# One queue for the reads of the transposed probabilities, and another place for the rounding of the mixed weights, in a fused attention and feed-forward kernel

## The chip, the cores and the metric

The kernel runs on one core of a Trainium2 chip. The metric is the time of one execution on the device, in microseconds, as the median of three runs: 532.76 us before the change, with runs from 532.27 to 533.12. All matrix products run on TensorE (PE). ScalarE (ACT), VectorE (DVE) and GpSimd (POOL) do the element-wise work, and SyncE (SP) issues most of the DMA transfers. ScalarE can issue transfers too, and does so in the kernel before.

## The reference

An attention with a global and a local window is followed by a gated feed-forward network of four weight matrices. In short (batch 4, 8 heads, 768 positions, 64 features a head; 8 global positions, a local window of 96):

```python
scores = matmul(q, k.T) / 8 + bias                      # bias = -slope(head) * distance
scores = where(is_global | is_local, scores, -1e9)      # local: 0 <= i - j < 96; global: j < 8
a = exp(scores - max(scores)); a = a / (sum(a) + 1e-9)
x = matmul(a, v)                                        # 4 x 8 x 768 x 64, laid out as 3072 x 512
h = ((x @ w1) * (x @ w2)) @ w3                          # 512 -> 1024 -> 1024
out = h @ w_out                                         # 1024 -> 512
```

## The kernel before

**Attention in 24 steps.** A step treats two head pairs of one block of 256 query positions; steps are counted from 0 to 23. In step s TensorE first makes a *visit*: the scores of step s (L488) and the products of the probabilities with the values of step s - 2 (L597). For each of the eight score tiles VectorE then subtracts the scores from the bias and takes the row extreme (L504), and ScalarE takes the exponential with the row sums (L505). These are the *rows* of the step. The scaling by the inverse sums follows: half of it on ScalarE (L521, four instructions a step) and half on VectorE (L523).

**The way of the probabilities.** The product with the values needs the probabilities transposed. VectorE transposes blocks of 32 x 32 (L558, four instructions a step), SyncE writes the result to device memory (`d`, L560, two transfers), and `back` (L568) reads it from there in four transfers into the tile `ph`, in an order that completes the transposition. Two of the four reads go out on SyncE's queue and two on ScalarE's. The reads of step s stand in step s + 1 in the program, and TensorE uses them in the visit of step s + 2. In the same place SyncE issues the loads for the next visit: keys and queries of step s + 1 (`qr`, L466) and values of step s - 1 (`vr`, L473). A buffer for a load comes free when TensorE has done the visit that used it, and SyncE waits for this with all that stands behind it in its queue.

**The feed-forward in slices.** TensorE's time between visits is filled with *slices* of `FeedForward.run`, a generator that the steps advance by fixed numbers (`SLICES`). For each eighth f of the 1024 features it makes two PSUM tiles, `m_f_0` and `m_f_1` (L220 to L222: weights and tokens are each split into a rounded high part and a rest, so one product takes three matmuls). ScalarE copies the first out of PSUM (L228), VectorE multiplies the second by it (L230), ScalarE rounds the product to its high part `gh` (L57), and VectorE subtracts to get the rest `gl` (L58). Then come the `o` tiles (L241 to L243), the copy of each out of PSUM (L251) and its store to the output (L252). All these PSUM tiles share two buffers: a tile can be begun when the tile before the last has been copied or multiplied out.

**The mixed weights.** The last part of the feed-forward (from about 400 us) is a Strassen product. It needs sums and differences of the weight blocks, which are prepared in the attention steps 7 to 22, one f in two steps: in an odd step `mix` forms them on GpSimd (L859, L862) into `tl`; in the following even step `round_off` rounds them on ScalarE to `th` (L867, 128 x 1024 elements) and subtracts on GpSimd (L869); and `keep` stores both to device memory (`tw`, L873, L874).

**What sets the order.** For the steps shown here the programs of TensorE, ScalarE, SyncE and GpSimd stand in the order in which the code is written. Only VectorE's order is made by a scheduler when the kernel is built, so it can change when another engine's code is moved. An instruction waits in its engine's queue for its inputs and for the buffer that it writes, with all behind it waiting too.

## Time and profile before

| | |
|---|---|
| median of three runs | 532.76 us (532.27 to 533.12) |
| the profiled execution | 532.92 us, of which the span of instructions is 531.2 us |
| TensorE matmuls (PE) | 520.4 us busy, 98% of the span, 4260 instructions |
| TensorE weight loads (PEld) | 414.1 us, beside the matmuls |
| VectorE (DVE) | 338.0 us, 64% |
| ScalarE (ACT) | 257.0 us, 48% |
| GpSimd (POOL) | 71.3 us, 13% |
| DMA | 107.7 MB, 203 GB/s in the mean |

A span is measured from the first to the last instruction of one profiled execution; the time of the execution is a little longer. Busy times are sums over the instructions of an engine. Times inside a trace count from the span's start. The granted TensorE clock stands at nine tenths or full speed in all 40 slices of the span, apart from one of eight tenths at the start.

Of the traffic in the attention steps, the page gives the median time from issue to landing: 3.4 us for the writes `d` (42 of them, 512 KB each), 6.7 us for the reads of `ph` on SyncE's queue and 6.2 us on ScalarE's (42 each, 160 KB), 4.5 us for the 16 `qr` loads of 624 KB and 6.1 us for the 17 `vr` loads of 512 KB.

### The profile page before, as it was taken

Reading aid. Unit: us, or ns where it says so; the run is one execution under the profiler, and the core shown is the slowest. Engines: PE = TensorE matmul, PEld = TensorE weight load, DVE = VectorE, ACT = ScalarE, POOL = GpSimd, SP = SyncE. Lnnn points to the kernel's source line nnn. Section 1 sums busy time; section 2 is a strip of 40 time slices with the busy share of each in tenths; the row PEclk is TensorE's granted clock in tenths of the full one; section 3 lists DMA queues with packets and bytes.
Section 4 is the critical chain, followed back from the end, with each engine's and each line's share of the span. In section 5 each row is a group of like instructions: output and inputs, shape, how many; then the busy total and the mean of one; then the engine's idle time right before and its main releaser. Section 6 shows DMA issues by size and latency. Waiting matters only on the chain.

```text
span 531.2 us, 11252 instructions
## 1 busy us (share of the span) xinstructions
PE 520.4 (98%) x4260; PEld 414.1 (78%) x4260; DVE 338.0 (64%) x906; ACT 257.0 (48%) x729; POOL 71.3 (13%) x87
## 2 busy tenths in 40 slices
PE   7999999999999999999999999999999999999996
PEld 3445468989988888888888888788888888888885
DVE  7999998976787576665767656677535433334400
ACT  0344776576676554546665554667424322222220
POOL 0000000000325050243214042412000000000000
PEclk9899999999999999999999999999999999999999
DMA  8977854477879765886767597988613322222031
GB/s 300 408 290 299 284 200 169 120 253 247 263 229 291 249 209 192 268 269 207 257 209 261 164 320 249 275 242 278 221 66 127 112 95 81 79 85 74 1 116 49
DMA packets 50653, 107.70 MB, mean 203 GB/s; under 512 B 4768, under 2 KB 28576, under 8 KB 50592
## 3 DMA queue, kind: packets, MB, share of 16 engines
q1 hardware_dynamic: 43056, 99.50, 54.3%
q10 hardware_dynamic: 7392, 6.88, 5.5%
q0 software_dynamic: 144, 0.52, 0.5%
q8 instruction: 35, 0.57, 0.4%
q14 instruction: 26, 0.21, 0.1%
HBM read 69.67 MB, written 36.70 MB: 200 GB/s over the span
## 4 chain that ended last, share of the span: by engine, by line
PE 84%; DVE 8%; DMA 4%; ACT 2%; issue 1%; SPq 0%; ACTq 0%; DVEq 0%
PE m L220 10%; PE m L221 9%; PE m L222 9%; PE a L948 8%; PE w L197 8%; PE o L241 6%; PE o L242 5%; PE o L243 5%; PE s L488 5%; PE v L597 5%; PE ob L968 4%; PE oa L968 4%; PE b L948 4%; PE c L948 2%; DVE t3s L164 2%; DMA ph<-d 2%
## 5 line engine op out<-in xcount | busy, mean ns | idle before, releaser
L220 PE MATMUL m<-xh,wqh 128*128 128x512 f32 (+1 forms) x320 | 113.3, 354 | 1.6 <-DVE ring_a L230 1.1
L221 PE MATMUL m<-xl,wqh 128*128 128x512 f32 (+1 forms) x320 | 111.0, 347 | 0.0
L222 PE MATMUL m<-xh,wql 128*128 128x512 f32 (+1 forms) x320 | 111.0, 347 | 0.0
L505 ACT ACTIVATE pr<-pr,mx 128x232 f32<-128x232 f32 (+1 forms) x192 | 88.1, 461 | 10.3 <-DVE mx L504 10.3
L220 PEld LDWEIGHTS m<-xh,wqh 128*128 128x128 f32 x320 | 60.5, 189 | 11.6 <-DVE ring_a L230 1.5
L504 DVE CUSTOM_DVE_ANT_0 pr<-s,biasw 128x232 f32<-128x232 f32 x160 | 54.0, 395 | 19.7 <-PE s L488 19.6
L222 PEld LDWEIGHTS m<-xh,wql 128*128 128x128 f32 x320 | 60.5, 189 | 7.6
L221 PEld LDWEIGHTS m<-xl,wqh 128*128 128x128 f32 x320 | 60.6, 189 | 7.1
L558 DVE STREAM_TRANSPOSE ph<-pr 128x512 f32<-128x512 f32 x84 | 49.1, 640 | 3.2 <-ACT pr L521 2.1
L241 PE MATMUL o<-wh,gh 128*128 128x512 f32 x128 | 50.8, 397 | 0.0
L243 PE MATMUL o<-wh,gl 128*128 128x512 f32 x128 | 49.9, 390 | 0.0
L242 PE MATMUL o<-wl,gh 128*128 128x512 f32 x128 | 49.9, 390 | 0.0
L57 ACT ACTIVATE gh<-ring_a 128x512 fp32r<-128x512 f32 x29 | 18.2, 629 | 50.8 <-DVE ring_a L230 48.0
L230 DVE TENSOR_TENSOR ring_a<-m,ring_a 128x512 f32<-128x512 f32 x32 | 21.8, 682 | 26.5 <-PE m L222 26.0
L869 POOL TENSOR_TENSOR tl<-tl,th 128x512 f32<-128x512 f32 x16 | 21.8, 1381 | 112.3 <-ACT th L867 112.3
L488 PE MATMUL s<-qr 64*64 64x168 f32 (+2 forms) x768 | 36.7, 299 | 0.0
L505 ACT ACTIVATION_READ_ACCUMULATOR pr<-pr,mx 128x1 f32 x192 | 36.1, 188 | 0.0
L597 PE MATMUL v<-ph,vr 64*64 64x64 f32 (+2 forms) x1208 | 34.5, 243 | 0.2 <-DMA ph<-d 0.2
L521 ACT ACTIVATE pr<-pr,sm 128x232 f32<-128x232 f32 (+1 forms) x84 | 33.2, 465 | 2.5 <-DVE sm L510 2.5
L597 PEld LDWEIGHTS v<-ph,vr 64*64 64x64 f32 (+1 forms) x1208 | 32.3, 133 | 1.7 <-DMA ph<-d 0.5
L197 PE MATMUL w<-wo,ta 128*128 128x512 f32 x64 | 30.2, 625 | 1.9 <-DVE ta L164 1.9
L523 DVE TENSOR_SCALAR pr<-pr,sm 128x232 f32<-128x232 f32 (+1 forms) x84 | 30.0, 398 | 1.3
(154 smaller groups left out, 850.3 us busy)
## 6 DMA issues: line engine op xcount, KB each, us to landing
d<-ph SPq DMA_DIRECT2D x42, 512.0 KB, 3.4
qr<-qk SPq DMA_DIRECT2D x16, 624.0 KB, 4.5
vr<-vx SPq DMA_DIRECT2D x17, 512.0 KB, 6.1
t<-tw SPq DMA_DIRECT2D x32, 256.0 KB, 3.0
ph<-d SPq DMA_DIRECT2D x42, 160.0 KB, 6.7
ph<-d ACTq DMA_DIRECT2D x42, 160.0 KB, 6.2
out_dram<-ring_o SPq DMA_DIRECT2D x24, 256.0 KB, 2.6
raw<-w3t SPq DMA_DIRECT2D x11, 512.0 KB, 9.6
```

The lines of the kernel that those rows point to most:

```text
L197: nc.tensor.matmul(ps, lhsT=x.bitcast(F32), rhs=self.wo[:, k].bitcast(F32), start=n == 0, stop=n == NFC - 1)
L220: nc.tensor.matmul(ps[:, z], lhsT=mh, rhs=xh[:, i], start=i == 0, stop=False)
L221: nc.tensor.matmul(ps[:, z], lhsT=mh, rhs=xl[:, i], start=False, stop=False)
L222: nc.tensor.matmul(ps[:, z], lhsT=ml, rhs=xh[:, i], start=False, stop=i == NCC - 1)
L241: nc.tensor.matmul(ps, lhsT=gh[:, f, ts], rhs=self.wh[:, f], start=f == 0, stop=False)
L242: nc.tensor.matmul(ps, lhsT=gh[:, f, ts], rhs=self.wl[:, f], start=False, stop=False)
L243: nc.tensor.matmul(ps, lhsT=gl[:, f, ts], rhs=self.wh[:, f], start=False, stop=f == NFC - 1)
L488: nc.tensor.matmul(ps[u][g * HQ:(g + 1) * HQ, j, cols], lhsT=m[:, q0:q0 + HQ], rhs=m[:, j * SLOT:][:, cols], start=True, stop=True)
L504: nc.vector.tensor_tensor_reduce(out=pr[:, j, u, w0:], in0=ps[u][:, j, w0:UW], in1=bias, scale=-SCALE, scalar=3.0e38, op0=ALU.add, op1=ALU ...
L505: nc.scalar.activation(pr[:, j, u, w0:], pr[:, j, u, w0:], AF.Exp, bias=m, scale=-1.0, accum_out=sm[:, j, u:u + 1])
L597: nc.tensor.matmul(uu[i][u * D:(u + 1) * D, j * P + q:j * P + q + n], lhsT=v[r], rhs=x[:, q // step:(q + n) // step][r], start=k == 0 and ...
L948: nc.tensor.matmul(ps, lhsT=a, rhs=b, start=first and k == 0 and i == 0, stop=k == HC - 1 and i == 2, skip_group_check=True)
```

## The change

Three things are done in the loop over the steps.

First, all four reads of `back` go out on SyncE's queue, and `back(s - 1)` stands ahead of the two `loads` instead of behind them. So in each step SyncE issues the reads of the transposed probabilities before anything else.

Second, `round_off` (ScalarE's rounding L867 and GpSimd's subtraction L869, in the even steps 8 to 22) stands behind `send`, which holds the transpositions, and no longer ahead of the first two slices of the step, which hold a copy L228 or L251 out of PSUM.

Third, `keep`, the stores of the mixed weights, stands one step later: in the odd step that follows, ahead of its slices, and so ahead of the `mix` that forms the next weights.

```diff
@@ back(s)
         for b, m0 in enumerate((1, 0, 3, 2)):
             ms = slice(m0, m0 + 5)
-            (nc.sync, nc.scalar)[b // 2].dma_start(out=x[b * BK:(b + 1) * BK].rearrange("r k a u c -> r (k a) (u c)")[:, ms], in_=d[:, :, :, b].rearrange("k a r e -> r (k a) e")[:, ms])
+            nc.sync.dma_start(out=x[b * BK:(b + 1) * BK].rearrange("r k a u c -> r (k a) (u c)")[:, ms], in_=d[:, :, :, b].rearrange("k a r e -> r (k a) e")[:, ms])
         phs[s] = x
@@ for s in range(SWAP + 1, n)
                     if i == 0 and uu is not None:
                         take(sv, uu)
+                back(s - 1)
                 loads(s + 1, vals=False)
                 loads(s - 1, keys=False)
-                back(s - 1)
-                if 0 <= s - MIX < 2 * NFC and (s - MIX) % 2:
-                    round_off()
+                f, late = divmod(s - MIX, 2)
+                if mixed and not late:
+                    keep()
                 slices(2)
                 for p, r in zip(pairs(s), rs):
                     softmax(*p, *r, nc.vector)
                 send(s, rs)
-                if mixed:
-                    keep()
-                if 0 <= s - MIX < 2 * NFC and (s - MIX) % 2 == 0:
-                    mix((s - MIX) // 2)
+                if mixed and late:
+                    round_off()
+                elif 0 <= f < NFC and not late:
+                    mix(f)
                 slices(SLICES[s] - 2)
```

What this does to the order of the instructions shows at four places. A row gives the line, the operation, what is written and read, the shape and how often it stands in a row; a number in a name counts tiles.

ScalarE in step 20, before, from the last exponentials on (`pr_0` and `pr_1` are the two head pairs of the step, `m_0_0` the first PSUM tile of the next group):

```order
L505 ACTIVATE pr_1_3770,sm_1_3772<-pr_1_3770,mx_1_3771 128x232 x4
L568 DMA ph_2_3651<-d_2_3652 32x5x256 x2
L867 ACTIVATE th<-tl 128x1024
L228 ACTIVATE ring_a<-m_0_0_3707 128x512
L521 ACTIVATE pr_0_3758<-pr_0_3758,sm_0_3760 128x232 x2
L521 ACTIVATE pr_1_3770<-pr_1_3770,sm_1_3772 128x232 x2
L57 ACTIVATE gh_3705<-ring_a 128x512
```

ScalarE at the same place, changed:

```order
L505 ACTIVATE pr_1_3770,sm_1_3772<-pr_1_3770,mx_1_3771 128x232 x4
L228 ACTIVATE ring_a<-m_0_0_3707 128x512
L521 ACTIVATE pr_0_3758<-pr_0_3758,sm_0_3760 128x232 x2
L521 ACTIVATE pr_1_3770<-pr_1_3770,sm_1_3772 128x232 x2
L867 ACTIVATE th<-tl 128x1024
L57 ACTIVATE gh_3705<-ring_a 128x512
L228 ACTIVATE ring_a<-m_1_0_3835 128x512
```

The two reads have left this queue, and the rounding L867 has moved from ahead of the copy L228 to behind the four scalings L521.

VectorE in the same step, before, from its half of the scalings on to the first row of step 21 (`pr_2`):

```order
L523 TENSOR_SCALAR pr_1_3770<-pr_1_3770,sm_1_3772 128x232 x2
L230 TENSOR_TENSOR ring_a<-m_0_1_3799,ring_a 128x512
L558 STREAM_TRANSPOSE ph_0_3818<-pr_0_3758 128x4x128 x2
L558 STREAM_TRANSPOSE ph_0_3818<-pr_1_3770 128x4x128 x2
L58 TENSOR_TENSOR gl_3706<-ring_a,gh_3705 128x512
L230 TENSOR_TENSOR ring_a<-m_1_1_3851,ring_a 128x512
L504 ISA pr_2_3911,mx_2_3912<-s_108,biasw 128x232
L504 ISA mx_2_3912 128x1
L58 TENSOR_TENSOR gl_3706<-ring_a,gh_3705 128x512
L504 ISA pr_2_3911,mx_2_3912<-s_109,biasw 128x232
```

VectorE at the same place, changed:

```order
L523 TENSOR_SCALAR pr_1_3770<-pr_1_3770,sm_1_3772 128x232 x2
L558 STREAM_TRANSPOSE ph_0_3815<-pr_0_3758 128x4x128 x2
L558 STREAM_TRANSPOSE ph_0_3815<-pr_1_3770 128x4x128 x2
L230 TENSOR_TENSOR ring_a<-m_0_1_3796,ring_a 128x512
L58 TENSOR_TENSOR gl_3706<-ring_a,gh_3705 128x512
L230 TENSOR_TENSOR ring_a<-m_1_1_3849,ring_a 128x512
L58 TENSOR_TENSOR gl_3706<-ring_a,gh_3705 128x512
L504 ISA pr_2_3909,mx_2_3910<-s_108,biasw 128x232
L504 ISA mx_2_3910 128x1
```

The product L230 of the tile `m_0_1` has moved from ahead of the four transpositions L558 to behind them. The second L58, which reads the ScalarE rounding L57 of the tile `m_1_1`, has moved from behind the first L504 of step 21 to ahead of it. The scheduler makes the first of these moves in steps 6, 10, 17, 20 and 21, and the second at the starts of the visits' rows in steps 6, 8, 17 and 21.

VectorE at the end of step 16 and the start of step 17 (`pr_2`), before:

```order
L230 TENSOR_TENSOR ring_a<-m_5_1_3189,ring_a 128x512
L504 ISA pr_2_3255,mx_2_3256<-s_108,biasw 128x232
L504 ISA mx_2_3256 128x1
L58 TENSOR_TENSOR gl_2812<-ring_a,gh_2811 128x512
L504 ISA pr_2_3255,mx_2_3256<-s_109,biasw 128x232
```

The same place, changed:

```order
L230 TENSOR_TENSOR ring_a<-m_5_1_3187,ring_a 128x512
L58 TENSOR_TENSOR gl_2810<-ring_a,gh_2809 128x512
L504 ISA pr_2_3253,mx_2_3254<-s_108,biasw 128x232
L504 ISA mx_2_3254 128x1
L504 ISA pr_2_3253,mx_2_3254<-s_109,biasw 128x232
```

The L58 of step 16 has moved past the first L504 of step 17 here as well.

SyncE from the writes of step 7 to the loads of step 8's end, before (`d` is the transposed tile in device memory, `ph` where it is read to, `tw` the stored mixed weights):

```order
L560 DMA d_2_1584<-ph_2_1583 128x1024 x2
L466 DMA qr_2_1724<-qk 128x1248
L473 DMA vr_2_1726<-vx 128x2x384
L568 DMA ph_2_1583<-d_2_1584 32x5x256 x2
L560 DMA d_0_1761<-ph_0_1760 128x1024 x2
L873 DMA tw<-th 128x1024
L874 DMA tw<-tl 128x1024
L252 DMA out_dram<-ring_o 128x512
L466 DMA qr_0_1865<-qk 128x1248
L473 DMA vr_0_1867<-vx 128x1024
L568 DMA ph_0_1760<-d_0_1761 32x5x256 x2
```

SyncE at the same place, changed:

```order
L560 DMA d_2_1584<-ph_2_1583 128x1024 x2
L568 DMA ph_2_1583<-d_2_1584 32x5x256 x4
L466 DMA qr_2_1728<-qk 128x1248
L473 DMA vr_2_1730<-vx 128x2x384
L560 DMA d_0_1758<-ph_0_1757 128x1024 x2
L252 DMA out_dram<-ring_o 128x512
L568 DMA ph_0_1757<-d_0_1758 32x5x256 x4
L466 DMA qr_0_1867<-qk 128x1248
L473 DMA vr_0_1869<-vx 128x1024
L873 DMA tw<-th 128x1024
L874 DMA tw<-tl 128x1024
```

The reads have moved ahead of the loads of keys and values and are four instead of two. The stores of the mixed weights, which stood behind the next writes, now stand behind the next loads. The first writes here end step 7 in the program, and the reads and loads directly behind them belong to step 8.

## Rows read from the trace of the kernel before

**Rows 1.** Waits of TensorE, 100 to 395 us (us, times, longest)

```profile
PE m L220 <- ACT ring_a L228: 0.5, 1, 0.5
PE m L220 <- DVE ring_a L230: 0.5, 1, 0.5
PE v L597 <- DMA ph<-d: 0.2, 1, 0.2
```

**Rows 2.** Timeline of TensorE, step 20 (start, duration, instruction, idle before)

```profile
333.72 0.39 PE L222 MATMUL m<-xh,wql 128*128 128x512 f32 x1
334.65 0.50 PE L220 MATMUL m<-xh,wqh 128*128 128x512 f32 x1 [0.55 <-ACT ring_a L228]
...
337.52 0.39 PE L220 MATMUL m<-xh,wqh 128*128 128x512 f32 x1
```

**Rows 3.** Timeline of TensorE, steps 21 and 22

```profile
351.06 0.39 PE L220 MATMUL m<-xh,wqh 128*128 128x512 f32 x1
...
353.13 0.39 PE L597 MATMUL v<-ph,vr 64*64 64x128 f32 x4
353.77 0.77 PE L597 MATMUL v<-ph,vr 40*64 40x128 f32 x24 [0.24 <-DMA ph<-d]
```

**Rows 4.** Timeline of ScalarE, step 20

```profile
333.08 1.04 ACT L867 ACTIVATE th<-tl 128x1024 fp32r<-128x1024 f32 x1
334.03 0.57 ACT L228 ACTIVATE ring_a<-m 128x512 f32<-128x512 f32 x1
334.50 1.61 ACT L521 ACTIVATE pr<-pr,sm 128x232 f32<-128x232 f32 x4
```

**Rows 5.** Timeline of VectorE, step 20

```profile
334.63 0.69 DVE L230 TENSOR_TENSOR ring_a<-m,ring_a 128x512 f32<-128x512 f32 x1 [0.42 <-ACT ring_a L228]
335.45 2.49 DVE L558 STREAM_TRANSPOSE ph<-pr 128x512 f32<-128x512 f32 x4
337.86 0.68 DVE L58 TENSOR_TENSOR gl<-ring_a,gh 128x512 fp32r<-128x512 f32 x1
```

**Rows 6.** Timeline of VectorE, end of step 16 and visit of step 17

```profile
285.77 0.40 DVE L504 CUSTOM_DVE_ANT_0 pr<-s,biasw 128x232 f32<-128x232 f32 x1
...
287.10 0.39 DVE L504 CUSTOM_DVE_ANT_0 pr<-s,biasw 128x232 f32<-128x232 f32 x1
```

**Rows 7.** Timeline of ScalarE, step 17

```profile
287.53 0.49 ACT L505 ACTIVATE pr<-pr,mx 128x232 f32<-128x232 f32 x1 [0.40 <-DVE mx L504]
...
291.81 1.62 ACT L521 ACTIVATE pr<-pr,sm 128x232 f32<-128x232 f32 x4
```

**Rows 8.** Timeline of TensorE, step 17

```profile
295.86 0.39 PE L220 MATMUL m<-xh,wqh 128*128 128x512 f32 x1
```

**Rows 9.** Timeline of ScalarE, step 21

```profile
347.22 1.62 ACT L521 ACTIVATE pr<-pr,sm 128x232 f32<-128x232 f32 x4
```

**Rows 10.** Timeline of ScalarE, step 10

```profile
184.78 1.05 ACT L867 ACTIVATE th<-tl 128x1024 fp32r<-128x1024 f32 x1
```

**Rows 11.** Timeline of TensorE, step 10

```profile
189.31 0.39 PE L220 MATMUL m<-xh,wqh 128*128 128x512 f32 x1
```

**Rows 12.** Timeline of SyncE's queue, step 8

```profile
151.22 0.81 SPq L560 DMA_DIRECT2D d<-ph  x2
```

**Rows 13.** DMA issues, 150.9 to 157 us (KB each, median us to landing)

```profile
d<-ph SPq DMA_DIRECT2D x2, 512.0 KB, 3.3
...
vr<-vx SPq DMA_DIRECT2D x1, 384.0 KB, 5.2
ph<-d SPq DMA_DIRECT2D x2, 160.0 KB, 4.9
ph<-d ACTq DMA_DIRECT2D x2, 160.0 KB, 5.1
```

**Rows 14.** Timeline of TensorE, visit of step 9

```profile
162.11 0.80 PE L488 MATMUL s<-qr 64*64 64x168 f32 x16
```

**Rows 15.** DMA issues of the whole execution

```profile
vr<-vx SPq DMA_DIRECT2D x8, 384.0 KB, 7.2
```

## The prediction, made before the changed kernel was run

> **What bounds the kernel now.** I read the list of waits of TensorE first. From 100 us to the end of the attention steps it names three waits, 0.5, 0.5 and 0.2 us [rows 1], and nothing else: TensorE runs almost without a hole, and the change can give back little. A matmul's end is modelled, so I take a hole from the starts of the matmuls, which normally follow each other by 0.23 us. In step 20 one stands at 333.72 and the next at 334.65 [rows 2]: a hole of 0.93 - 0.23 = 0.70 us. In step 22 the product with the values stops between a group of four at 353.13 and one of 24 at 353.77 [rows 3]; the 24 follow each other by 0.77/24 = 0.03, so four of them end at 353.26, and the hole is 0.51 - 0.03 = 0.48 us, behind the reads of the transposed probabilities. The third (L220 behind DVE L230) is in step 7, where neither ScalarE nor VectorE gets another order; I leave it as it is.
>
> Then the timelines of ScalarE and VectorE around these holes. In step 20 ScalarE rounds the mixed weights from 333.08 for 1.04 us, and only then copies the PSUM tile that TensorE waits for, at 334.03 [rows 4]. So both edits aim at a hole that exists. What is to be seen next is VectorE: L230 multiplies the second half of each tile pair out of PSUM, and TensorE may write the next-but-one tile only after it. In this kernel there are two such PSUM buffers, so each L230 has a time by which it must end.
>
> **The change part by part.** *The rounding moved behind the scaling (8 times).* In step 20 the copy L228 starts where the rounding stood, 333.08, and ends 0.57 later, 333.65. TensorE is free at 333.72 + 0.23 = 333.95, so the hole of 0.70 closes. The same edit moves VectorE, whose order the scheduler makes anew: at five places L230 now stands behind the four transpositions and no longer ahead of them (steps 6, 10, 17, 20 and 21). The price of this is the heart of the sum. The four transpositions take 335.45 to 337.86 = 2.41 us until the next instruction starts, and L230 takes 0.69 [rows 5]. The first transposition needs two of the four scalings L521; the four take 1.61 us [rows 4], the longer ones on this engine 0.48 each, so they start 0.38 apart and the second ends 0.86 after the first starts. A hand-over between engines is 0.03 to 0.05 (ScalarE's L228 ends at 334.60, VectorE's L230 starts at 334.63, TensorE at 334.65); I use 0.04 and, for TensorE, 0.05.
>
> - Step 20: L521 starts 0.47 behind L228 as before, 333.55; the second ends at 334.41; transpositions from 334.45; L230 from 336.86 to 337.55; TensorE's next tile pair half can start at 337.60. Undisturbed it would start 2.87 (337.52 - 334.65, rows 2) behind 333.95, at 336.82. So a new hole of 0.78 opens, and against 337.52 before the step loses 0.08. The gain of 0.70 is spent three microseconds later.
> - Step 17: here nothing is rounded, but another move counts. The subtraction L58 of step 16 stood between the first and the second L504 of step 17 and now stands ahead of both, and it waits for ScalarE's L57: the first L504 goes from 285.77 to where the second stood, 287.10 [rows 6]. ScalarE's first exponential then starts where the second did, 287.53, and the whole row of them moves by one, 0.49 [rows 7]. The second L521 ended at 291.81 + 0.86 = 292.67, now 293.16; transpositions from 293.20; L230 from 295.61 to 296.30; TensorE 296.35, where its matmul stood at 295.86 [rows 8]: 0.49 lost.
> - Step 21: the same two moves. Second L521 until 347.22 + 0.86 = 348.08 [rows 9], plus 0.49 for one exponential, as in step 17, plus the 0.08 of step 20: 348.65. Transpositions from 348.69, L230 from 351.10 to 351.79, TensorE 351.84; undisturbed 351.06 + 0.08 = 351.14 [rows 3]: 0.70 lost.
> - Step 10: the rounding starts at 184.78 [rows 10] and leaves its place to L228, so L521 starts at 185.25, its second ends at 186.11; transpositions from 186.15, L230 from 188.56 to 189.25, TensorE at 189.30 against 189.31 [rows 11]: it just fits. Step 6 has a whole visit of scores between the two tiles, and nothing is late.
>
> In the other steps with a rounding, ScalarE does the same work in front of its next copy in another order, and that copy comes when it came; GpSimd's subtraction follows the rounding later, and the stores of the mixed weights go out one step later, in the odd steps behind the loads. The weights formed next wait for these stores, but ScalarE asks for them a whole step further on. I cost this at nothing; if that cover were gone, ScalarE would wait at the rounding with its next copy queued behind it.
>
> *The reads on one queue and first.* Per step two reads leave ScalarE's queue. They overlap its arithmetic, so I count no time on ScalarE. On SyncE the four reads now go as soon as the two writes have landed, ahead of both loads, which earlier waited for TensorE to free their buffers. So the reads of step 21 no longer end at the visit of step 22, and 0.48 comes back. What they are moved past is the two loads for the next visit. They are late only where the writes land after the loads' buffers are free, in the short steps; the tightest is step 8. Its two writes are issued from 151.22 on, 0.81 for both [rows 12], so the second at some 151.6, and land 3.3 later [rows 13], 154.9. Four reads by the same 0.41 each put the keys' load at 156.6 and the values' at 157.0, 0.4 behind it. TensorE's visit begins at 162.11 [rows 14] and uses the values some 0.7 later, 162.8. From its issue to its landing the values' load took 5.2 in this very step [rows 13]: 162.2, in time by 0.6. The median of such loads over the kernel is 7.2 [rows 15], and then it lands at 164.2, 1.4 late. I take the nearer row, so 0, and keep 1.4 as the far end; the keys are issued earlier and wanted only 0.7 earlier, and stand no worse. Nothing excludes a small gain from the transfers that no longer overlap; the holes that they could close are in the sum already.
>
> The Trainium skill, DMA: Bandwidth & Descriptors, section Issuing engines are not separate DMA queues, says that transfers from any issuing engine run on the same 16 DMA engines and interleave, and that a second issuing engine saves only issue time. By it the single queue costs nothing but issue. The same page's section Queues, rings and completion order says that each DMA engine takes turns between the queues that have work; that speaks against the change, since reads that leave ScalarE's queue lose their own turn and line up with the loads. The trace agrees with the first: in step 8 the two reads from SyncE's queue took 4.9 in the median and the two from ScalarE's, issued at the same time, 5.1 [rows 13]. By the first the sum stays as it is; by the second the loads would be later by the issue of two reads, 0.8 us: 163.0, or 0.2 on the sum, on the way to rival 3.
>
> Sum: +0.08 (step 20) + 0.49 (step 17) + 0.70 (step 21) - 0.48 (step 22) = +0.79 us. The profiled execution took 532.92 us, 531.2 of it span; it would take 533.7. It lies 0.16 above the median of the runs, 532.76, and on that median I predict 533.6. A measurement of this kernel can tell about 0.2%, 1.07 us, from no change, so this is no difference that shows.
>
> **Rivals.**
> 1. The holes go and no new one opens: 0.70 + 0.48 = 1.18 less, 531.6. For it: both holes have the cause that the edits remove, and step 10 shows a moved L230 that still fits. Against it: in steps 17 and 21 the second L521 would have to end 0.5 and 0.7 earlier than its rows allow. 0.13.
> 2. Half of it: the L58 that now stands ahead of the first L504 hides beside ScalarE's queue. Then steps 17 and 21 lose 0 and 0.70 - 0.49 = 0.21, and the sum is 0.08 + 0.21 - 0.48 = -0.19: 532.6. Against it: the second exponential of step 17 starts 0.04 behind the second L504 [rows 6, 7], so ScalarE has nothing to hide it behind. 0.10.
> 3. Slower: in step 8 the loads stand behind all four reads in one queue, and the values come late for the visit at 162.11. It decides once they land more than 5.8 behind their issue (162.8 - 157.0). Price up to 1.4; I take 1.0, as the median holds for half of such loads, on top of the sum: 534.6. For it: the median of 7.2 [rows 15] is above 5.8. Against it: the 5.2 of this step [rows 13] is below. 0.20.
>
> **How the numbers follow.** Forecast 0.57, rivals 0.13, 0.10 and 0.20. Of the forecast 0.07 falls beyond 533.83 by scatter of the small holes, of rival 1 0.03 falls inside 0.2%. Faster: 0.10. Same: 0.50 + 0.03 + 0.10 = 0.63. Slower: 0.07 + 0.20 = 0.27. The forecast's own range is 533.0 to 534.2. The range leaves out the far part of rival 1 and what rival 3 costs at its dearest: 531.8 to 534.8.
>
> **What would show it.** Right: TensorE has no hole at 333.7, but one of some 0.8 near 336.8, behind L230; one of 0.5 near 295.9 and one of 0.7 near 351.2, each with L230 directly behind four transpositions; the product with the values of step 22 without a wait; the hole of step 7 as before. Wrong: L230 of steps 17 and 21 ending before TensorE wants the tile (then rival 1 or 2), or a wait of the visit at 162 for a load (rival 3), or new holes in steps that this working does not name.

## The result and the profile after

The changed kernel took 535.76 us in the median (534.73 to 537.65, 6 runs), the kernel before on the same chip 532.78 (531.92 to 533.12, 6 runs): a ratio of 1.0062, with a 95% interval of 1.0048 to 1.0076. It is slower by 3.0 us. The forecast was 533.6 with a range to 534.8: its sum had the right sign, and called it too small to be told from no change; it is three to four times that sum.

The page of the profiled execution (534.73 us):

```profile
span 533.0 us, 11178 instructions
...
PE 519.5 (97%) x4260; PEld 412.5 (77%) x4260; DVE 332.6 (62%) x906; ACT 257.0 (48%) x729; POOL 71.6 (13%) x87
```

TensorE's waits from 100 to 395 us, which answer to [rows 1]:

```profile
PE m L220 <- DVE ring_a L230: 2.2, 4, 0.8
PE v L597 <- DMA vr<-vx: 0.3, 1, 0.3
```

The four waits for L230 are those of steps 7, 17, 20 and 21; ScalarE's L228 and the reads of `ph` have left the list, and a load of values has come into it.

TensorE around the three new holes (steps 17, 20 and 21), which answer to [rows 2, 3, 8]; start, duration, instruction, idle time before:

```profile
296.20 0.39 PE L222 MATMUL m<-xh,wql 128*128 128x512 f32 x1
296.92 0.50 PE L220 MATMUL m<-xh,wqh 128*128 128x512 f32 x1 [0.33 <-DVE ring_a L230]
```

```profile
337.70 0.39 PE L222 MATMUL m<-xh,wql 128*128 128x512 f32 x1
338.90 0.50 PE L220 MATMUL m<-xh,wqh 128*128 128x512 f32 x1 [0.81 <-DVE ring_a L230]
```

```profile
352.34 0.39 PE L222 MATMUL m<-xh,wql 128*128 128x512 f32 x1
353.33 0.50 PE L220 MATMUL m<-xh,wqh 128*128 128x512 f32 x1 [0.60 <-DVE ring_a L230]
```

By the starts, less 0.23, the holes are 0.49, 0.97 and 0.76 us. The prediction had 0.49, 0.78 and 0.70, at these places. A fourth one, too short for the list, stands in step 10: 0.32 between the starts before rounding, so 0.09:

```profile
189.28 0.39 PE L222 MATMUL m<-xh,wql 128*128 128x512 f32 x1
189.59 0.50 PE L220 MATMUL m<-xh,wqh 128*128 128x512 f32 x1
```

VectorE in step 20, which answers to [rows 5]:

```profile
335.77 2.49 DVE L558 STREAM_TRANSPOSE ph<-pr 128x512 f32<-128x512 f32 x4 [0.29 <-ACT pr L521]
338.19 0.66 DVE L230 TENSOR_TENSOR ring_a<-m,ring_a 128x512 f32<-128x512 f32 x1
```

L230 stands behind the four transpositions and ends at 338.85; TensorE's next matmul starts at 338.90. The step runs 1.27 us later than before at its start; less that, L230 starts at 336.92, where the prediction had 336.86.

SyncE in step 8, which answers to [rows 12], and TensorE at the visit of step 9, which answers to [rows 14]:

```profile
150.70 0.81 SPq L560 DMA_DIRECT2D d<-ph  x2
154.82 1.76 SPq L568 DMA_DIRECT2D ph<-d  x4
156.68 0.38 SPq L466 DMA_DIRECT2D qr<-qk  x1
157.16 0.55 SPq L473 DMA_DIRECT2D vr<-vx  x1
```

```profile
161.27 0.39 PE L243 MATMUL o<-wh,gl 128*128 128x512 f32 x1
161.79 0.80 PE L488 MATMUL s<-qr 64*64 64x168 f32 x16
162.90 0.77 PE L597 MATMUL v<-ph,vr 64*64 64x128 f32 x23 [0.31 <-DMA vr<-vx]
```

The same places before the change:

```profile
153.32 0.33 SPq L466 DMA_DIRECT2D qr<-qk  x1
153.83 0.55 SPq L473 DMA_DIRECT2D vr<-vx  x1
155.53 0.81 SPq L568 DMA_DIRECT2D ph<-d  x2
```

```profile
161.79 0.39 PE L243 MATMUL o<-wh,gl 128*128 128x512 f32 x1
```

The loads of keys and values, which left 2.0 and 2.5 us behind the start of the visit of step 8 before (153.32 and 153.83, from 151.31), now leave 5.9 and 6.4 behind it (from 150.79): they stand behind four reads, and these wait until 154.77 for the second write to land. The keys come 0.2 us late for the visit: before, its first L488 started 0.32 behind the last L243 (161.79 and 162.11), now 0.52. The values come 0.5 late behind that.

TensorE in the visit of step 22, which answers to [rows 3]:

```profile
354.92 0.80 PE L488 MATMUL s<-qr 64*64 64x168 f32 x16
355.54 0.85 PE L597 MATMUL v<-ph,vr 64*64 64x128 f32 x32
```

The 32 products with the values follow without a break; the hole of 0.48 is not there.

Where the time went can be read from the starts of the visits (the first L488 of each), since TensorE's program between two of them is the same. The second column is of another profile of the kernel before, taken in the experiments:

| from visit to visit | before, as shown | before, second profile | changed | changed less second |
|---|---|---|---|---|
| 8 to 9 (late keys) | 10.80 | 10.79 | 11.00 | +0.21 |
| 9 to 10 (late values) | 16.26 | 16.26 | 16.77 | +0.51 |
| 10 to 11 | 16.47 | 16.48 | 16.72 | +0.24 |
| 17 to 18 | 15.11 | 15.12 | 15.74 | +0.62 |
| 20 to 21 | 13.04 | 13.07 | 13.28 | +0.21 |
| 21 to 22 | 12.18 | 12.19 | 13.08 | +0.89 |
| 22 to 23 | 13.08 | 12.48 | 12.50 | +0.02 |
| all from 4 to 23 | 261.60 | 261.04 | 263.94 | +2.90 |

These stretches hold 2.70 of the 2.90 us; the rest is in pieces of 0.06 or less. The sum fits the 3.0 us between the medians. Against the profile that the prediction had, the difference is 0.56 smaller, and that lies in the visit of step 22. Ahead of the visit of step 4 and behind that of step 23 the profiles differ too, by up to 1.2 and 0.9 us, two profiles of one kernel among them, so whole spans compare less well than this stretch.

### The profile page after: what moved, and what is told of

Read it like the earlier page. It is cut to its first block, busy times and chain, and to the rows that moved or that the text cites. A ratio compares the mean times of both kernels' runs of the same rounds, so it can differ in the third digit from the quotient of the medians.

```text
span 533.0 us, 11178 instructions
## 1 busy us (share of the span) xinstructions
PE 519.5 (97%) x4260; PEld 412.5 (77%) x4260; DVE 332.6 (62%) x906; ACT 257.0 (48%) x729; POOL 71.6 (13%) x87
## 4 chain that ended last, share of the span: by engine, by line
PE 72%; DVE 16%; DMA 4%; ACT 4%; issue 2%; SPq 1%; DVEq 0%; ACTq 0%
PE m L220 9%; PE m L221 8%; PE m L222 8%; PE a L949 8%; PE o L241 5%; PE o L242 5%; PE o L243 5%; PE v L597 4%; PE ob L969 4%; PE oa L969 4%; PE b L949 4%; PE s L488 4%; ACT pr L505 2%; PE c L949 2%; DVE t3s L164 2%
## 5 line engine op out<-in xcount | busy, mean ns | idle before, releaser
L504 DVE CUSTOM_DVE_ANT_0 pr<-s,biasw 128x232 f32<-128x232 f32 x160 | 53.8, 395 | 23.6 <-PE s L488 23.6
L558 DVE STREAM_TRANSPOSE ph<-pr 128x512 f32<-128x512 f32 x84 | 49.2, 642 | 2.2 <-ACT pr L521 1.9
L243 PE MATMUL o<-wh,gl 128*128 128x512 f32 x128 | 49.8, 389 | 0.0
L57 ACT ACTIVATE gh<-ring_a 128x512 fp32r<-128x512 f32 x29 | 18.3, 631 | 54.0 <-DVE ring_a L230 54.0
L488 PE MATMUL s<-qr 64*64 64x168 f32 (+2 forms) x768 | 36.5, 299 | 0.1
L230 DVE TENSOR_TENSOR ring_a<-m,ring_a 128x512 f32<-128x512 f32 x32 | 21.7, 679 | 23.7 <-PE m L222 23.6
L521 ACT ACTIVATE pr<-pr,sm 128x232 f32<-128x232 f32 (+1 forms) x84 | 33.3, 466 | 1.9 <-DVE sm L510 1.9
L197 PE MATMUL w<-wo,ta 128*128 128x512 f32 x64 | 28.9, 599 | 3.0 <-DVE ta L164 2.2
L58 DVE TENSOR_TENSOR gl<-ring_a,gh 128x512 fp32r<-128x512 f32 x29 | 21.7, 747 | 15.4 <-ACT gh L57 15.4
L488 PEld LDWEIGHTS s<-qr 64*64 64x64 f32 x768 | 24.2, 133 | 7.1 <-issue 6.0
```

The source lines that it names most:

```text
L243: nc.tensor.matmul(ps, lhsT=gl[:, f, ts], rhs=self.wh[:, f], start=False, stop=f == NFC - 1)
L488: nc.tensor.matmul(ps[u][g * HQ:(g + 1) * HQ, j, cols], lhsT=m[:, q0:q0 + HQ], rhs=m[:, j * SLOT:][:, cols], start=True, stop=True)
L504: nc.vector.tensor_tensor_reduce(out=pr[:, j, u, w0:], in0=ps[u][:, j, w0:UW], in1=bias, scale=-SCALE, scalar=3.0e38, op0=ALU.add, op1=ALU ...
L558: nc.vector.transpose(x[:, k, :, u1 - 4 + u0:u1], units[:, u0:, k0:k0 + P].rearrange("p u (b c) -> p b u c", c=BK))
```

## The experiments

The theory after the comparison: two things cost the time, VectorE's place for L230 (steps 10, 17, 20 and 21, some 2 us) and the loads behind the reads in step 8 (0.7 us or more). The rivals: the run-to-run difference of the start, the single queue as such, and the third part of the change, the later stores, which the prediction had priced at nothing. All times are medians of single executions; each kernel ran beside the kernel before, e1 to e4, e5 to e8 and e9 to e12 on one chip each. The medians of before there were 532.12, 532.10 and 532.17. Of the three the changed kernel ran on the first alone (e1), so what is said of e7 to e9 and e12 against its 535.41 goes from chip to chip.

| run | what | median (range, runs) | ratio to before (95%) |
|---|---|---|---|
| e1 | changed, again | 535.41 (534.56 to 535.45, 5) | 1.0054 (1.0041 to 1.0067) |
| e2 | changed, loads first in step 8 | 534.35 (533.34 to 534.78, 5) | 1.0041 (1.0028 to 1.0054) |
| e3 | reads moved alone | 534.89 (534.31 to 535.77, 6) | 1.0051 (1.0039 to 1.0064) |
| e4 | rounding and stores moved alone | 533.53 (532.30 to 536.34, 12) | 1.0030 (1.0015 to 1.0044) |
| e5 | before, again | 532.44 (531.08 to 533.36, 12) | 1.0002 (0.9992 to 1.0013) |
| e6 | before, two places changed | 531.17 (530.17 to 532.90, 12) | 0.9982 (0.9969 to 0.9994) |
| e7 | changed, reads on two queues | 533.67 (532.05 to 537.25, 12) | 1.0037 (1.0016 to 1.0057) |
| e8 | changed, loads first in four steps | 535.37 (534.40 to 537.12, 6) | 1.0062 (1.0041 to 1.0083) |
| e9 | changed, L230 first in four steps | 533.63 (532.84 to 535.93, 12) | 1.0031 (1.0019 to 1.0043) |
| e10 | rounding moved, stores with it | 530.83 (530.47 to 532.29, 12) | 0.9979 (0.9969 to 0.9989) |
| e11 | stores moved alone | 533.94 (533.07 to 535.43, 11) | 1.0032 (1.0021 to 1.0044) |
| e12 | e2 and e9 together | 531.52 (530.73 to 532.90, 11) | 0.9985 (0.9976 to 0.9994) |

**e1, the changed kernel again** (no edit).

> The changed kernel once more, for a second profile. Its six runs spread over 2.9 us (534.7 to 537.7), those of before over 1.2, and the first profile is of the fastest. Theory A: the loads that now stand behind the four reads land late by an amount that differs from run to run. Then a second profile has the same three holes behind VectorE's L230 (near 296, 338 and 352 us, 0.5, 1.0 and 0.8 us, each within 0.1), and all that differs lies in the visits that wait for a load: the one near 162 us (0.9 in the first profile), and those near 139 and 367, where the values landed only 0.5 and 0.7 us ahead of their use. Rival B: what differs is the start of the program (before 100 us) or the clock; then the waits of these visits are as in the first profile.

The profile (534.90 us) has the same three holes, 0.49, 0.96 and 0.76, and the same waits near 162 (0.14 for the keys and 0.52 for the values; 0.20 and 0.51 in the first). The small hole of step 10 is 0.18 and not 0.09. The visit of step 4 starts at 103.36 and not at 103.48. The visits near 139 and 367 wait for nothing. So the waits repeat; what makes the spread is not in it, for 534.90 lies low among all eleven runs of this kernel (534.56 to 537.65).

**e2, the loads first in step 8 alone**, against the changed kernel.

```diff
-                back(s - 1)
+                if s != 8:
+                    back(s - 1)
                 loads(s + 1, vals=False)
                 loads(s - 1, keys=False)
+                if s == 8:
+                    back(s - 1)
```

> The changed kernel, but in step 8 alone the two loads stand ahead of the four reads again. Theory A: the visit near 162 us waits for nothing, and 0.9 us or more come back: a median 0.9 to 2.0 below that of the changed kernel, some 534 to 535, still above before. The holes behind L230 stay. Rival C: the loads are late because all reads share one queue and its transfers, wherever they stand in it; then the visit waits as before, or the reads of step 7 become late instead, and the time is that of the changed kernel within 0.4 us.

TensorE's waits in this kernel:

```profile
PE m L220 <- DVE ring_a L230: 2.2, 4, 0.8
```

No visit waits for a load, and 1.06 us come back in the median; the intervals of e1 and e2 overlap, so the time alone would not carry it. e12 against e9, which differ by the same edit and ran on one chip, gives 2.1 us with intervals apart. All four reads still share one queue here, so rival C falls: it is their place ahead of the loads that costs.

**e3, the reads moved alone**, against the kernel before.

```diff
-            (nc.sync, nc.scalar)[b // 2].dma_start(out=x[b * BK:(b + 1) * BK]...
+            nc.sync.dma_start(out=x[b * BK:(b + 1) * BK]...
...
+                back(s - 1)
                 loads(s + 1, vals=False)
                 loads(s - 1, keys=False)
-                back(s - 1)
```

> Only the reads are moved (one queue, ahead of the loads); the rounding and the stores of the mixed weights are where they were. VectorE's order then has L230 behind the transpositions in steps 6, 10, 17 and 21, but not in step 20. Theory A plus the order of VectorE: holes of 0.5 near 296 and 0.8 near 352, the wait near 162, the old hole of 0.70 in step 20, no wait in step 22: 0.6 + 0.9 + 0.9 + 0.2 (step 10) - 0.6 = +2.0 us on the profile, and up to 1 more in the median: a ratio of 1.004 to 1.006. Rival D, that the rounding's move causes the new holes, as the prediction had it: no hole near 296 and 352, and the time is that of before plus the 0.9 of step 8 less 0.5, within 0.5 us of before.

```profile
PE m L220 <- DVE ring_a L230: 2.0, 3, 0.8
PE m L220 <- ACT ring_a L228: 0.6, 1, 0.6
PE v L597 <- DMA vr<-vx: 0.3, 1, 0.3
```

The time is 2.8 us above before. L230 makes a hole of 0.90 in step 10 and one of 0.96 in step 21, step 20 keeps its old one for L228, and the values of step 8 are late. In step 17 there is none, though I expected it and L230 stands behind the transpositions there as well:

```profile
293.69 2.49 DVE L558 STREAM_TRANSPOSE ph<-pr 128x512 f32<-128x512 f32 x4 [0.15 <-ACT pr L521]
296.10 0.65 DVE L230 TENSOR_TENSOR ring_a<-m,ring_a 128x512 f32<-128x512 f32 x1
```

In this kernel L58 of step 16 is not moved ahead of the first L504, so L230 ends 0.12 earlier, and the step runs 0.42 later; TensorE wants the tile at 296.85, and L230 is done at 296.75. Both moves are needed for the hole of step 17, as the prediction had worked it out: here L230 is moved without L58, in e9 L58 without L230, and neither has it. Rival D falls: the reads alone move L230, not the rounding.

**e4, the rounding and the stores moved alone**, against the changed kernel.

```diff
-            nc.sync.dma_start(out=x[b * BK:(b + 1) * BK]...
+            (nc.sync, nc.scalar)[b // 2].dma_start(out=x[b * BK:(b + 1) * BK]...
...
-                back(s - 1)
                 loads(s + 1, vals=False)
                 loads(s - 1, keys=False)
+                back(s - 1)
```

> Only the rounding and the stores of the mixed weights are moved; the reads are as before, and VectorE's order is that of before. Theory: the hole of 0.70 us in step 20 goes, with the 0.11 by which the first matmul behind a hole starts the next one later, and nothing else changes, the hole of 0.48 in step 22 included: -0.8 us, a ratio of 0.9985. Rival E: the later rounding delays L57 and with it L58 and the o tiles, or GpSimd's subtraction runs into other VectorE work, and new holes of as much appear in even steps: a ratio of 1.000 or more.

Step 20's hole is gone, and yet the kernel is 1.4 us slower than before, with the widest spread but one (e7). TensorE now waits 1.0 us in step 22, for the reads:

```profile
PE v L597 <- DMA ph<-d: 1.0, 1, 1.0
PE m L220 <- DVE ring_a L230: 0.5, 1, 0.5
PE v L597 <- DVE mx L504: 0.4, 1, 0.4
```

The third wait is at the visit of step 7, ahead of the first moved instruction; the last of its reads had landed just before it ended (139.80 and 139.94). The theory had counted on step 22's wait as it was, 0.48; neither had it grow. The time is that of rival E, but its holes in the even steps are not there; e10 and e11 separate what is left.

**e5, the kernel before again** (no edit).

> The kernel before once more, for a second profile: the one shown took 532.92 us, while 12 of 17 later runs took 532.0 to 532.3. Theory: the shown profile lost some 0.5 us ahead of the attention steps (in all five other profiles the second visit of the trace begins 0.4 to 0.7 us earlier, with the same program up to there), so the new profile has its second visit near 103.4 and a time near 532.2, with the holes of steps 7, 20 and 22 as before. Rival: the wait of the visit near 139 us, seen in the kernel with the rounding alone (0.64), differs from run to run before as well and makes the difference; then it shows in slower runs only, and the start is as in the shown profile.

The visit of step 4 starts at 102.82, 1.17 us earlier than in the profile shown; some 0.6 had been expected. And TensorE's waits are these:

```profile
PE m L220 <- ACT ring_a L228: 0.6, 1, 0.6
PE m L220 <- DVE ring_a L230: 0.5, 1, 0.5
```

The wait for `ph` is missing. In the visit of step 22 the products stand without a break, as they do in the changed kernel:

```profile
351.38 0.80 PE L488 MATMUL s<-qr 64*64 64x168 f32 x16
352.00 0.85 PE L597 MATMUL v<-ph,vr 64*64 64x128 f32 x32
```

So the hole of 0.48 in [rows 3] stands in one of two profiles of the same kernel; that execution was 0.5 us above the median here.

**e6, two places alone**, against the kernel before. The rounding of step 20 behind `send`, with its stores in the same step; the reads ahead of the loads in step 21, on two queues.

```diff
+                if s == 21:
+                    back(s - 1)
                 loads(s + 1, vals=False)
                 loads(s - 1, keys=False)
-                back(s - 1)
-                if 0 <= s - MIX < 2 * NFC and (s - MIX) % 2:
+                if s != 21:
+                    back(s - 1)
+                late = 0 <= s - MIX < 2 * NFC and (s - MIX) % 2
+                if late and s != 20:
                     round_off()
...
                 send(s, rs)
+                if late and s == 20:
+                    round_off()
                 if mixed:
                     keep()
```

> The kernel before with the rounding behind the scalings in step 20 alone (its stores right behind it, in the same step as before), and the reads ahead of the loads in step 21 alone, on two queues as before; VectorE's order is exactly that of before. Theory: the holes of steps 20 and 22 go, each with 0.11 for the restart, and no new one opens: 0.81 + 0.59 = 1.4 us less, a ratio of 0.9974. Rival F: as with the rounding alone, what step 20 gives is taken back at the visit near 352, since the reads of step 21 land when the DMA engines are through with the loads, wherever the issues stand: then the time is that of before within 0.3 us.

0.93 us below before, beyond the interval of no change. Only step 7's wait is left in its trace (0.5 for L230), so rival F falls. The expected 1.4 counted step 22's hole in.

**e7, the reads on two queues**, two on SyncE's ahead of the loads, against the changed kernel.

```diff
-            nc.sync.dma_start(out=x[b * BK:(b + 1) * BK]...
+            (nc.sync, nc.scalar)[b // 2].dma_start(out=x[b * BK:(b + 1) * BK]...
```

> The changed kernel, but the four reads go out on two queues as before (two on SyncE's, ahead of the loads, two on ScalarE's). VectorE's order is that of before. Theory: no new hole behind L230 in steps 10, 17, 20 and 21, no old one in step 20, and two reads ahead of the loads instead of four leave the values 0.8 us more in step 8: no wait there. 1.4 us less than before at best, a ratio of 0.9975, and 4 less than the changed kernel. Rival G: the stores of the mixed weights, which now stand in the odd steps next to the reads and loads, make some of these land late, as in the kernel with the rounding alone, which spread from 532.3 to 536.3: then the runs spread by 2 us or more, and the median lies between 532 and 534, above before.

No hole behind L230 in steps 10, 17, 20 and 21. But loads and reads are late at the visits of steps 8, 9 and 22, and the runs spread over 5 us. SyncE ahead of the visit of step 8:

```profile
138.03 0.81 SPq L560 DMA_DIRECT2D d<-ph  x2
144.29 0.80 SPq L568 DMA_DIRECT2D ph<-d  x2
145.20 0.37 SPq L466 DMA_DIRECT2D qr<-qk  x1
145.68 0.55 SPq L473 DMA_DIRECT2D vr<-vx  x1
```

The second write was issued at 138.47 and landed at 144.16, and the reads wait for it. The loads behind them left 6.7 and 7.2 us behind the start of the visit of step 7 (138.47); in the profile shown of before it was 2.0 and 2.7 (141.21 and 141.89, from 139.23). The visit of step 8 waited for both. That only two reads stand ahead of the loads did not help there: what counted was the wait for the write. In step 8 it was another thing. The loads left earlier than in the changed kernel, 4.5 and 4.9 us behind the start of the visit and not 5.9 and 6.4, but took 6.8 and 7.3 us to land and not 5.0 and 5.5, beside the two reads on ScalarE's queue. Time and spread are as rival G had them, and in step 21 ScalarE's reads go out behind the stores (345.59, the second store 345.01) and hold up the visit of step 22; but the losses of steps 7 and 8 stand ahead of the first store that was moved, so its cause is a part only.

**e8, the loads first in steps 5, 6, 8 and 22**, against e2.

```diff
-                if s != 8:
+                if s not in (5, 6, 8, 22):
...
-                if s == 8:
+                if s in (5, 6, 8, 22):
```

> The changed kernel, but in steps 5, 6, 8 and 22 the two loads stand ahead of the four reads. With step 8 alone the time was 534.35 (533.3 to 534.8) against 535.41, and its profile, the fastest of its runs, showed no late load. Theory A: in the slower runs it is the visits near 127, 139 and 367 that wait, where loads stood 0.5 to 2.4 us ahead of their use; then the median comes near the fastest run, 533.3, with a spread under 0.7 us. Rival H: the spread has nothing to do with these loads; then median and spread stay, 534.3 and 1.4.

Its profile shows no late load, as e2's, and the median does not fall: 535.37, with a spread of 2.7. Theory A falls, and so does rival H as it was put, for it had e2's 534.3 and 1.4. Nothing in the profile accounts for 1.0 us above e2: from visit to visit it is 0.4 slower, 0.3 of it in step 10. So the price of step 8 rests on the profiles, on e2 and on e12 against e9, and not on e8; what sets the spread is left open.

**e9, L230 ahead of the transpositions in steps 10, 17, 20 and 21**, against the changed kernel.

```diff
-            nc.vector.tensor_tensor(out=a, in0=ps, in1=a, op=ALU.mult)
+            self.mul = nc.vector.tensor_tensor(out=a, in0=ps, in1=a, op=ALU.mult)
...
-                send(s, rs)
+                k = 2
+                if s in (10, 17, 20, 21):
+                    mul = ff.mul
+                    while ff.mul is mul:
+                        slices(1)
+                        k += 1
+                    with tc.issue_after(ff.mul.ins):
+                        send(s, rs)
+                else:
+                    send(s, rs)
...
-                slices(SLICES[s] - 2)
+                slices(SLICES[s] - k)
```

> The changed kernel, but in steps 10, 17, 20 and 21 VectorE takes the product L230 ahead of the four transpositions, as before; the reads stay on one queue and ahead of the loads (ScalarE takes the rounding behind L57 in steps 10 and 20, nothing else differs). Theory: the place of L230 alone makes the holes of these steps, so 0.24 + 0.62 + 1.08 + 0.89 = 2.8 us go, the wait of step 8's loads stays: 1.5 to 2.8 below the changed kernel (535.4), some 532.6 to 533.9. Rival I: the holes stand where they are, since the transpositions or TensorE wait for something else there (the earlier scalings, the reads on SyncE's queue): 535.4 within 0.5.

1.8 us below the changed kernel, and the holes behind L230 of these steps are gone; rival I falls. The waits at the visit of step 9 stay (0.30 and 0.55 against the second profile of before). In its profile step 22 has a new hole of 0.60 behind ScalarE's copy L228 (361.42 to 362.25), and new waits stand at the visit of step 23, for the loads of step 22, which TensorE now reaches earlier (the keys are late by 0.30: 364.90 to 365.52, less the usual 0.32). From visit to visit it is 1.5 below the changed kernel.

**e10, the rounding behind the transpositions in all eight steps, the stores in the same step**, against the kernel before.

```diff
-                if 0 <= s - MIX < 2 * NFC and (s - MIX) % 2:
-                    round_off()
+                late = 0 <= s - MIX < 2 * NFC and (s - MIX) % 2
...
                 send(s, rs)
+                if late:
+                    round_off()
                 if mixed:
                     keep()
```

> The rounding behind the transpositions in all eight steps, its stores right behind it in the same step (in the change they stand one step later); the reads as before, VectorE's order as before. The kernel with the rounding alone, which had the stores one step later, took 533.53 and spread from 532.3 to 536.3. Theory J: the later stores of 512 KB, next to the reads and loads, made that: then this one has step 20's hole closed and loses nothing, 0 to 0.8 below before, a ratio of 0.9985 to 1.000, with the spread of before. Theory K: it is the rounding's own place; then it is slower than before as that one was, by some 1.0 us or more.

1.3 us below before, the lowest median here; e6, which moves the rounding in step 20 alone, lies within its interval. TensorE's waits:

```profile
PE m L220 <- DVE ring_a L230: 0.5, 1, 0.5
```

Only step 7's is left, and step 20 is 0.89 us shorter than in the second profile of before. Theory J holds: the rounding's own move is a gain, of more than the 0.8 that was expected.

**e11, the stores one step later and nothing else**, against the kernel before.

```diff
                 back(s - 1)
+                if mixed and (s - MIX) % 2 == 0:
+                    keep()
...
                 send(s, rs)
-                if mixed:
-                    keep()
```

> The kernel before with the stores of the mixed weights one step later, directly behind the loads and reads, and nothing else moved; every engine but SyncE has exactly the order of before. Theory J: the 512 KB then cross the reads and loads of the odd steps: +0.5 to 2 us in the median, a wider spread, and waits for ph or vr in the visits of even steps, 353 above all. Theory K: nothing hangs on these stores: a ratio of 1.000 within 0.1%.

1.8 us slower than before. SyncE in step 21 and TensorE in the visit of step 22:

```profile
342.29 0.33 SPq L466 DMA_DIRECT2D qr<-qk  x1
342.80 0.69 SPq L473 DMA_DIRECT2D vr<-vx  x1
343.60 1.05 SPq L568 DMA_DIRECT2D ph<-d  x2
344.70 0.43 SPq L873 DMA_DIRECT2D tw<-th  x1
345.17 0.43 SPq L874 DMA_DIRECT2D tw<-tl  x1
```

```profile
353.08 0.39 PE L597 MATMUL v<-ph,vr 64*64 64x128 f32 x4
354.48 0.77 PE L597 MATMUL v<-ph,vr 40*64 40x128 f32 x24 [1.01 <-DMA ph<-d]
```

Two stores of 512 KB now go out beside the reads: ScalarE's two took 8.8 us in the median, against 7.1 in the second profile of before and 8.2 in the one shown, and TensorE waits 1.3 us for them. Theory J holds again. Another 0.58 us of this profile stands at the visit of step 7, ahead of the first store that was moved.

**e12, e2 and e9 together**: both of their edits in one kernel.

> The changed kernel with both repairs: L230 ahead of the transpositions in steps 10, 17, 20 and 21, and the loads ahead of the reads in step 8 alone. If these two are all that the change costs, what is left is its gain, step 20's hole of 0.81: 531.3 to 532, at or below before (532.1). If the later stores cost more (theory J), it stays at 532.5 to 533.5, above before, with a spread of 2 us or more.

531.52: 0.65 us below before, as expected, and 3.9 below the changed kernel, 1.0 more than the 1.8 and 1.1 of each alone. So these two are what the change costs, and in the median the later stores cost little or nothing in it. The profiled execution took 532.90, the longest of the eleven, and has waits at the visit of step 23:

```profile
363.78 0.39 PE L222 MATMUL m<-xh,wql 128*128 128x512 f32 x1
364.96 0.80 PE L488 MATMUL s<-qr 64*64 64x168 f32 x16 [0.79 <-DMA qr<-qk]
366.27 0.45 PE L597 MATMUL v<-ph,vr 64*64 64x128 f32 x6 [0.51 <-issue]
```

The keys alone cost 0.84 us there. In step 22 they went out behind reads that waited for a write which took 5.2 us to land, against 3.6 in the second profile of before; the two stores were still under way when it was issued. That the stores slowed it is not shown. The wait makes 0.84 of the 1.4 us by which this execution lies above the median; whether the shorter ones have it is not known.

## Why the prediction was wrong

**The size failed at three terms; the mechanism of the forecast and that of rival 3 both came.**

1. *Step 8, put at 0.* This is the step that failed most, 0.72 us. The sentence "issued from 151.22 on ... and land 3.3 later" took the median of two writes [rows 13]; the reads wait for the second, which lands later. In the very profile that the prediction had it took 3.79 us from its issue (151.66 to 155.44, and the first read of before follows at 155.53), in the changed kernel 3.65 (151.13 to 154.77). That is 0.4 us. The four reads took 1.86 us to the keys' issue and not 1.64, which is 0.2; the values followed the keys by 0.48 and not 0.4, which is 0.1; their load took 5.50 and not 5.2, 0.3; and the first product started 0.25 behind its landing (162.66 to 162.90), for which the sum had nothing. Together 1.2, and the margin was 0.6, or 0.5 with the use at 162.73 and not 162.8. "The keys ... stand no worse" was wrong too; they were the first to be late. Rival 3 named mechanism, place and price; the 1.0 that it took was a little dear, and its chance of 0.20 hung on the same margin. The "nearer row" was indeed the nearer; the margin could not carry the other numbers that went into it.

2. *Step 22, credited with 0.48.* The hole went, as said. But by e5 the kernel before does not have it in every execution. The profiled execution was 0.16 us above the median of three runs; against the later medians of before, 532.1 to 532.4, it was 0.5 to 0.8 above. The holes of steps 7 and 20, behind instructions, are the same to 0.01 us in both profiles of before. That is no rule: step 10's in the changed kernel, also behind an instruction, is 0.09 in one profile and 0.18 in the other.

3. *Step 10, "it just fits", and the restarts.* Step 10 lost 0.24. The margin there was 0.01, and in the changed kernel ScalarE came to the copy 6.54 us behind the start of the visit, where it had come to the rounding at 6.41 before. Behind each of these holes the first matmul starts the next one 0.34 us later and not 0.23 (338.90 to 339.24 in step 20): 0.11 that the prediction did not count, in steps 10, 17, 20 and 21; another 0.02 to 0.06 goes in the ten matmuls that follow. With it the holes of 0.09, 0.49, 0.76 and 0.97 become the losses of the table: 0.24, 0.62, 0.89, and 0.21 in step 20, where the old hole and its restart, together 0.89 by e10, go.

With the measured stretches for these terms the sum reads 0.21 (step 20) + 0.62 (step 17) + 0.89 (step 21) + 0.02 (step 22) + 0.24 (step 10) + 0.72 (step 8) = 2.70, against 0.79.

**What was right.** The places of the three holes, their sizes to within 0.2 us, and the cause: e9 puts L230 back, the holes go and 1.8 us are gained. The share of L58 in step 17 was right as well, by e3 and e9. **What was right for a wrong reason:** "the same edit moves VectorE" put the new order down to the rounding. In e4 and e10, where the rounding alone moves, L230 stands where it stood; in e3, where the reads alone move, it is behind the transpositions in steps 6, 10, 17 and 21. In e7, with the reads first but on two queues, it stands where it stood: so it is the two reads' leaving ScalarE's queue that moves it. Only step 20 needs the rounding's move as well.

**The stores, "I cost this at nothing; if that cover were gone".** In the changed kernel they cost little or nothing in the median (e12), and the cover that was named holds in the changed kernel's trace: the wait for the stores of step 21 falls on GpSimd, 11.6 us ahead of an L862 at 354.55, GpSimd is done with the weights at 357.47, and ScalarE rounds them at 362.86. But alone the later stores cost 1.8 us (e11), by another way than a wait of ScalarE: the reads of step 21 come late for the visit of step 22. In e4, e7 and e11 ScalarE's two reads go out there after at least one of the stores and land after 7.5 to 9.0 us (7.1 and 8.2 in the two profiles of before, without the stores); in the changed kernel all four go out ahead of the stores and land after 2.7 to 5.4. That this place is what protects them is read from these landings; no run moves the stores alone in the changed kernel.

**The rule on queues.** The loads left SyncE 3.9 us later behind the start of the visit, because an instruction ahead of them in its queue waited for a write; with two queues (e7) the same happened in step 7. The Trainium skill, DMA: Bandwidth & Descriptors, section Issuing engines are not separate DMA queues, says that a second issuing engine saves issue time only. No run here isolates that for the transfers: in step 8 of e7, with two reads on the other queue, the loads took 1.8 us longer to land than in the changed kernel. And it is not the point here: what an engine's queue decided is who stood behind whose wait. Rates and issue times, which the prediction weighed, say nothing on that.

**What is open.** The runs of one kernel spread over 1 to 5 us, those of the kernel before over 1.6 to 2.8 on one chip. The start up to the visit of step 4 differs by up to 1.2 us between profiles, and landings differ by 2 us (the values' load of step 7 took 7.56 and 5.51 in the two profiles of before). Two profiles are of long executions, the one shown of before and e12's: the first has a late start and step 22's hole, the second the waits of step 23. Whether such waits make the spread of the other kernels, e8's above all, was not seen. Why the scheduler moves L230 when reads leave ScalarE was not tried either.

A version that beats both kernels came out of it: e10, which keeps the reads as they were and moves only the rounding, with its stores, 530.83 us.

## What to carry to other kernels

Before an instruction that waits is put ahead of others in a queue, give each of those the landing time that it now inherits, from the last transfer it waits for and not from a median, and hold its margin against the spread of such landings. Look at how a scheduler reorders an engine that the edit does not touch: here that cost more than all the edits gave (1.8 us by e9, against 1.3 for the rounding's move in e10). Of a hole behind a DMA, or of a margin near nothing, look in a second profile whether it is there.

## What was not expected of the hardware

Equal reads (160 KB each) land after 3.4 us in the median where all other transfers stand behind them (step 8 of the changed kernel), and after 8.8 behind two loads and beside two stores of 512 KB (step 21 of e11; without the stores, in the two profiles of before, 8.2 and 7.1):

```profile
ph<-d SPq DMA_DIRECT2D x4, 160.0 KB, 3.4
```

```profile
tw<-th SPq DMA_DIRECT2D x1, 512.0 KB, 7.7
tw<-tl SPq DMA_DIRECT2D x1, 512.0 KB, 8.8
...
ph<-d ACTq DMA_DIRECT2D x2, 160.0 KB, 8.8
```

And a hole in TensorE cost 0.11 us beyond its length, by the start of the second matmul behind it: with tiles of 512 columns 0.34 us behind the first and not 0.23, in step 20 of both kernels and in steps 10, 17 and 21 of the changed one.
